# SyncE's transfers in the program's order, the first tables behind a GpSimd copy, bias rows that don't overlap

## The chip, the core and the metric

One core of a Trainium2 chip runs the whole program. It has TensorE (PE, matmuls into PSUM), VectorE (DVE), ScalarE (ACT), GpSimd (POOL) and SyncE (SP); each takes its instructions in the order in which they stand in its queue. SP and POOL here issue most transfers (DMAs) between the large memory and the core's own memory (SBUF); 16 DMA engines carry them. The metric is device time of one execution in microseconds.

## The reference

Three blocks follow one another on a tensor x of 4 x 3072 x 256 in float32.

```
X = rfft(x, axis=1)                       # over the 3072 positions
Yr = Xr @ w_r - Xi @ w_i + b_r ;  Yi = Xr @ w_i + Xi @ w_r + b_i
Yr, Yi = soft_threshold(Yr, 0.01), soft_threshold(Yi, 0.01)
y = irfft(Yr + 1j*Yi, n=3072, axis=1)

x_prev = y shifted by one position (first row zero)
xk = mu_k*y + (1-mu_k)*x_prev ;  xr = mu_r*y + (1-mu_r)*x_prev
z = sigmoid(xr @ w_r2) * (relu(xk @ w_k)**2 @ w_v)     # 256 -> 1024 -> 256

h = z @ w_in ;  out = (h * clip(h+3, 0, 6) / 6) @ w_out   # 256 -> 2048 -> 256
```

## The kernel before

Each float32 operand is split into a rounded high part (ACT copies it, line 147) and a remainder (DVE subtracts, line 148), and three matmuls per product (line 156) keep the precision.

The transform is done as 96 x 32. For batch b there are four stages. `s1(b)` has eight steps: each takes two chunks of x (96 partitions x 512 numbers, line 255), multiplies them by a 96 x 96 table `f1`, copies the sums out of PSUM on ACT (`s1sb`, line 290) and stores them to a scratch tensor `sc_a` (line 291). `mid(b)` has 12 groups j: `s2(j)` reads a chunk of `sc_a` and multiplies by a table `tt` (for j = 0 also by `tex`), `mix(j)` applies `w_r` and `w_i` (held in `aw`), adds `bias` and applies the threshold on DVE (lines 361 to 363), `ia(j)` goes back by another table and stores to `sc_b` (line 379). `ib(b)` has eight steps: they read `sc_b`, multiply by `fi` and store to `sc_y` (line 426). Chunks go through a ring of five buffers `a`; `fetch` splits up to four chunks ahead of their use and loads up to four ahead of the split. Tables come through `load_t` (line 310) on POOL's queue, into three buffers.

Then come 24 tiles of 512 positions of the second block: `load_y` loads a tile `yt` (line 489), `prep` mixes it with its shifted copy by `mus` and `omu` (lines 506 and 511), then the units `u_r`, `u_k`, `u_v`. These tiles are interleaved with the transform of later batches through `feed`. The third block follows, again in 24 tiles. Weights are loaded in pieces by `load` (line 181) and decoded on ACT and DVE in small steps by `decoder`.

The order of the work at the start is a list of parts in `first`: `s1` of batch 0 (steps 0 to 7 of the enumeration at line 814), two steps of `s1` of batch 1 (8 and 9), `mid` of batch 0 (10 to 33), five more steps of `s1` of batch 1, and two steps of `ib` of batch 0. After step 7 the loop loads `w_r` and `w_i`, the second table, and calls `vectors`, which loads the bias and the two mu vectors and computes `omu = 1 - mu`.

The tile framework keeps the order of the program text on the engines that are in the set `order` (line 126). Before, that set names PE, ACT, DVE and POOL; SP's instructions are put in an order by the framework's planner.

The bias tile is 128 partitions x 3 x 256: partition rows 0 to 63 take b_r three times, 64 to 127 b_i three times, and then row 64, slot 0, is written again with b_r (line 476).

Of the kernel before, what the change touches and what calls it, by code (L numbers as in the profile page):

```python
# [9 lines left out]
F32 = mybir.dt.float32  # L10
# [4 lines left out]
ALU = mybir.AluOpType  # L15
# [3 lines left out]
B, S, D = 4, 3072, 256  # L19
# [84 lines left out]
def fourier_mix_ffn_kernel(  # L104
# [18 lines left out]
):  # L123
    nc = tc.nc
    EN = mybir.EngineType
    order = {EN.PE, EN.Activation, EN.DVE, EN.Pool}

    dram = ctx.enter_context(tc.tile_pool(name="dram", bufs=1, space=DRAM))
    sc_a = [dram.tile([N1, N2, D], F32, name=f"sc_a{b}") for b in range(B)]
# [7 lines left out]
    cst = ctx.enter_context(tc.tile_pool(name="cst", bufs=1))  # L137
# [4 lines left out]
    def ptile(name):  # L142
        return ps.tile([128, 1024], F32, tag="h", name=name)
# [6 lines left out]
    def three(o, pairs, first=True, last=True, **kw):  # L150

        n = 3 * len(pairs)
        i = 0
        for (lh, ll), (rh, rl) in pairs:
            for a, c in ((lh, rh), (ll, rh), (lh, rl)):
                nc.tensor.matmul(o, a, c, start=first and i == 0, stop=last and i == n - 1, **kw)  # L156
                i += 1
# [70 lines left out]
    with tc.manual_schedule(engines=order):  # L228
# [6 lines left out]
        mus = cst.tile([128, 2, 2], F32, name="mus")  # L235
        omu = cst.tile([128, 2, 2], F32, name="omu")
        half = cst.tile([128, 1], F32, name="half")
        top = cst.tile([128, 2, 1], F32, name="top")
        bias = fp.tile([128, 3, D], F32, name="bias")
        tex = fp.tile([128, 2, 64], F32R, name="tex")  # L240
# [28 lines left out]
        def take(n):  # L269

            u = head["use"]
            load_chunks(u + n)
            split_chunks(u + n)
            r = [live.pop(u + i) for i in range(n)]
            head["use"] = u + n
            return r

        def fetch():

            split_chunks(head["use"] + 4)  # L280
            load_chunks(head["split"] + 4)

        def s1(b, lo, hi):
            for s in range(lo, hi):
                p = ptile("s1")
                flat = lambda t: t.rearrange("p n d -> p (n d)")
                for i, (h, l) in enumerate(take(2)):
                    three(p[:N1, 512 * i : 512 * i + 512], [((f1[:, 0], f1[:, 1]), (flat(h), flat(l)))])
                sb = fp.tile([128, 4, D], F32, tag="ev", bufs=3, name="s1sb")
                nc.scalar.activation(flat(sb[:N1]), p[:N1], AF.Copy)  # L290
                nc.sync.dma_start(out=sc_a[b][:, 4 * s : 4 * s + 4], in_=sb[:N1])
                if s == 7:
                    ready.add(("a", b))
                    if b == 0:
                        nc.gpsimd.dma_start(out=tex, in_=ext)
                        load_t(0, 0)
                fetch()
                yield
# [4 lines left out]
        def load_t(b, j):  # L303

            if j >= NP + 2:
                b, j = b + 1, j - NP - 2
            if b < B:
                t = fp.tile([128, 2, 640], F32R, tag="t", bufs=3, name="tt")
                c = slice(0 if j < NP else 384, 640 if j >= 2 else 384)
                nc.gpsimd.dma_start(out=t[:, :, c], in_=tab[j, :, :, c])  # L310
                tt[b, j] = t
# [125 lines left out]
        def plan(kind, b, lo=0, hi=0):  # L437
            if kind == "s1":
                v = x[b].rearrange("(p n) d -> p n d", n=N2)
                chunks.extend((v[:, 2 * c : 2 * c + 2], None, N1) for c in range(2 * lo, 2 * hi))  # L440
                return kind, s1(b, lo, hi)
            if kind == "mid":
                v = sc_a[b].rearrange("(j g c) n d -> j (c n) g d", g=2, c=4)
                chunks.extend((v[j], ("a", b), 128) for j in range(NP))
                return kind, mid(b)
            for c in CHUNKS[lo:hi]:
                chunks.extend((sc_b[b][:, n : n + 2], ("b", b), N1) for n in (4 * c, 4 * c + 2))
            return kind, ib(b, lo, hi)
# [22 lines left out]

        def vectors():
            for i, v in enumerate((b_r, b_i)):
                rows = v.partition_broadcast(64).unsqueeze(1).to_broadcast([64, 3, D])
                nc.sync.dma_start(out=bias[64 * i : 64 * i + 64], in_=rows)
            nc.sync.dma_start(out=bias[64:65, 0], in_=b_r.partition_broadcast(1))
            with nc.allow_non_contiguous_dma(reason="two vectors"):
                for i, m in enumerate((mu_k, mu_r)):
                    nc.sync.dma_start(out=mus[:, i], in_=m.rearrange("(a p) -> p a", p=128))
            nc.vector.tensor_scalar(omu, mus, -1.0, 1.0, op0=ALU.mult, op1=ALU.add)  # L480


        seq = [(b, t) for b in range(B) for t in (1, 2, 3, 4, 5, 0)]
# [314 lines left out]
        def stream(parts):  # L798

            for kind, part in parts:  # L800
                if kind == "ib":
                    if ends:
                        for _ in range(2):
                            ends.pop(0)()
                            yield
                        for _ in range(3):
                            fetch()
                            yield
                for _ in part:
                    if ends:  # L810
                        ends.pop(0)()
                    yield

        for step, _ in enumerate(stream(first)):
            if step == LOAD_MIX:
                plain = [(w, w.load(stage1, *job[1:]), job[1:]) for w in aw for job in w.jobs]
                load_t(0, 1)
                vectors()
            if step in SPLIT_MIX:
                w, staged, job = plain.pop(0)  # L820
                for _ in w.decode(staged, *job):
                    pass
            if step == LOAD_FI:
                nc.gpsimd.dma_start(out=fi.rearrange("p s n -> p (s n)"), in_=small[:, 2 * N1 : 4 * N1])
            if step in DECODE:
                next(loads, None)
# [159 lines left out]
```

## Time and profile before

| what | value |
|---|---|
| median of 3 runs | 2081.03 us (2080.89 to 2084.46) |
| the profiled execution | 2082.47 us, span 2080.7 us |
| TensorE busy | 1992.8 us, 96% of the span |
| VectorE, ScalarE busy | 1549.8 us, 1323.2 us |
| mean granted clock | 0.976 of full speed |

The profiled execution lasts 1.77 us longer than the span of its trace, and 1.44 us longer than the median of the runs. Busy time is a sum over stages: a stage in which TensorE works all the time and the start, in which it often waits, are in the same number, so the rows below go by stretches of the span.

### The profile page before, as it was taken

Reading aid. Unit: us, or ns where it says so; the run is one execution under the profiler, and the core shown is the slowest. Engines: PE = TensorE matmul, PEld = TensorE weight load, DVE = VectorE, ACT = ScalarE, POOL = GpSimd, SP = SyncE. Lnnn points to the kernel's source line nnn. Section 1 sums busy time; section 2 is a strip of 40 time slices with the busy share of each in tenths; the row PEclk is TensorE's granted clock in tenths of the full one; section 3 lists DMA queues with packets and bytes.
Section 4 is the critical chain, followed back from the end, with each engine's and each line's share of the span. In section 5 each row is a group of like instructions: output and inputs, shape, how many; then the busy total and the mean of one; then the engine's idle time right before and its main releaser. Section 6 shows DMA issues by size and latency. Waiting matters only on the chain.

```text
span 2080.7 us, 33798 instructions
## 1 busy us (share of the span) xinstructions
PE 1992.8 (96%) x13928; PEld 1844.5 (89%) x13928; DVE 1549.8 (74%) x1975; ACT 1323.2 (64%) x1917; POOL 35.0 (2%) x63
## 2 busy tenths in 40 slices
PE   6878999999999999889998999999999999999998
PEld 4867998898789888667787999999999999999998
DVE  3868667777677686767777777877787778777875
ACT  5556447555754565555646777777777777667775
POOL 0000000000000000000000000000000000000000
PEclk7978999999999999999999999999999999999999
DMA  9765447543653352122100001100110011001100
GB/s 265 240 205 165 123 114 228 163 142 115 216 170 111 95 179 65 63 75 77 51 31 24 29 23 29 32 21 23 30 32 21 22 31 32 21 22 31 32 11 21
DMA packets 106988, 175.85 MB, mean 85 GB/s; under 512 B 12945, under 2 KB 63314, under 8 KB 106834
## 3 DMA queue, kind: packets, MB, share of 16 engines
q1 hardware_dynamic: 96034, 141.76, 22.1%
q0 software_dynamic: 10480, 31.67, 5.7%
q8 instruction: 109, 1.79, 0.4%
q14 instruction: 45, 0.37, 0.1%
q10 hardware_dynamic: 320, 0.26, 0.0%
HBM read 110.35 MB, written 63.31 MB: 83 GB/s over the span
## 4 chain that ended last, share of the span: by engine, by line
PE 76%; DVE 14%; ACT 6%; issue 2%; DMA 2%; SPq 0%; ACTq 0%; DVEq 0%
PE oacc L776 24%; PE rq L776 15%; PE acc L156 8%; PE pk L156 7%; PE cc L776 6%; PE mix L156 5%; PE s L156 4%; DVE g L552 2%; DVE gl L553 2%; PE pr L156 2%; DVE xf L511 1%; PE ia L156 1%; DVE kl L518 1%; PE ib L421 1%; PE ib L420 1%
## 5 line engine op out<-in xcount | busy, mean ns | idle before, releaser
L776 PE MATMUL oacc<-wo_hi,gl 128*128 128x256 f32 x1536 | 426.7, 278 | 0.6 <-DVE gl L750 0.6
L776 PE MATMUL oacc<-wo_hi,gh 128*128 128x256 f32 x1536 | 427.1, 278 | 0.0
L776 PE MATMUL oacc<-wo_lo,gh 128*128 128x256 f32 x1536 | 425.4, 277 | 0.0
L776 PEld LDWEIGHTS oacc<-wo_hi,gl 128*128 128x128 f32 x1536 | 288.7, 188 | 1.0 <-DVE gl L750 0.8
L776 PEld LDWEIGHTS oacc<-wo_hi,gh 128*128 128x128 f32 x1536 | 288.5, 188 | 0.2
L776 PEld LDWEIGHTS oacc<-wo_lo,gh 128*128 128x128 f32 x1536 | 288.7, 188 | 0.0
L732 DVE TENSOR_TENSOR c<-rq,s 128x512 f32<-128x512 f32 x184 | 127.3, 692 | 184.2 <-ACT s L728 184.2
L745 DVE SCALAR_TENSOR_TENSOR g<-g,c 128x1024 f32<-128x1024 f32 x184 | 225.5, 1226 | 27.1 <-ACT g L744 17.4
L749 ACT ACTIVATE gh<-g 128x1024 fp32r<-128x1024 f32 x184 | 195.2, 1061 | 55.8 <-DVE g L745 55.8
L750 DVE TENSOR_TENSOR gl<-g,gh 128x1024 fp32r<-128x1024 f32 x184 | 223.7, 1216 | 1.2 <-ACT gh L749 1.2
L776 PE MATMUL rq<-th,sw 128*128 128x256 f32 x1104 | 217.4, 277 | 7.3 <-DVE g L606 7.3
L744 ACT ACTIVATE g<-c,half 128x1024 f32<-128x1024 f32 x184 | 211.5, 1150 | 4.1 <-DVE c L733 1.4
L712 ACT ACTIVATE s<-rq 128x512 f32<-128x512 f32 x184 | 109.9, 598 | 112.0 <-PE rq L776 111.5
L776 PEld LDWEIGHTS rq<-th,sw 128*128 128x128 f32 x1104 | 166.4, 188 | 7.5 <-DVE g L606 7.5
L156 PE MATMUL acc<-gl,wv_hi 128*128 128x512 f32 x384 | 153.8, 400 | 13.3 <-DVE gl L553 13.3
L547 ACT ACTIVATE g<-pk 128x1024 f32<-128x1024 f32 x96 | 97.6, 1016 | 106.5 <-PE pk L156 106.4
L156 PE MATMUL pk<-kh,wk_hi 128*128 128x512 f32 x384 | 152.8, 398 | 9.3 <-ACT kh L517 5.2
L776 PE MATMUL rq<-tl,sw 128*128 128x256 f32 x552 | 153.9, 279 | 2.8 <-DVE tl L679 2.8
L148 DVE TENSOR_TENSOR al<-a,ah 96x512 fp32r<-96x512 f32 (+1 forms) x176 | 114.9, 684 | 55.2 <-ACT ah L147 55.2
L156 PE MATMUL acc<-gh,wv_hi 128*128 128x512 f32 x384 | 153.2, 399 | 1.6 <-ACT gh L551 1.5
L156 PE MATMUL acc<-gh,wv_lo 128*128 128x512 f32 x384 | 152.2, 396 | 0.0
L156 PE MATMUL pk<-kl,wk_hi 128*128 128x512 f32 x384 | 151.9, 396 | 0.0
(150 smaller groups left out, 4953.0 us busy)
## 6 DMA issues: line engine op xcount, KB each, us to landing
tt<-in_tab_dram POOLq DMA_DIRECT2D x40, 640.0 KB, 4.9
yt<-sc_y SPq DMA_DIRECT2D x23, 608.0 KB, 3.9
a<-in_x_dram SPq DMA_DIRECT2D x64, 192.0 KB, 3.5
sc_a<-s1sb SPq DMA_DIRECT2D x32, 384.0 KB, 3.9
a<-sc_a SPq DMA_DIRECT2D x48, 256.0 KB, 3.2
sc_b<-iasb SPq DMA_DIRECT2D x48, 256.0 KB, 4.8
a<-sc_b SPq DMA_DIRECT2D x64, 192.0 KB, 3.1
sc_y<-ysb SPq DMA_DIRECT2D x32, 384.0 KB, 2.9
```

What stands on the lines that cost most here:

```text
L148: nc.vector.tensor_sub(l, src, h.bitcast(F32))
L156: nc.tensor.matmul(o, a, c, start=first and i == 0, stop=last and i == n - 1, **kw)
L547: nc.scalar.activation(g, p, AF.Relu)
L552: nc.vector.tensor_mul(g, g, g)
L553: nc.vector.tensor_sub(l, g, h.bitcast(F32))
L712: nc.scalar.activation(s[:, 1:3].rearrange("p a n -> p (a n)"), rq, AF.Copy)
L732: nc.vector.tensor_add(c[:, 1::2], two(rq), s[:, 0:2])
L744: nc.scalar.activation(g, c, AF.Relu, bias=half, scale=1.0 / 6.0)
L745: nc.vector.scalar_tensor_tensor(g, g, 1.0, c, op0=ALU.min, op1=ALU.mult)
L749: lambda: nc.scalar.activation(h, g, AF.Copy),
L750: lambda: nc.vector.tensor_sub(l, g, h.bitcast(F32)),
L776: return lambda: nc.tensor.matmul(o, lhs, rhs, start=start, stop=stop, skip_group_check=True)
```

## The change

It edits five places.

1. SP joins the set `order`, so its transfers are issued in the order of the program text, in the whole kernel.
2. In step 4 of `s1` of batch 0, POOL copies one number of the step's output `s1sb` into a new tile `hold`. In POOL's order this copy stands ahead of the transfers of `tex` and of the first three tables, and behind that of `f1`.
3. The bias is written in four transfers that don't overlap: slots 1 and 2 of the two halves, then slot 0 of rows 0 to 64 with b_r and of rows 65 to 127 with b_i.
4. `omu` is computed at step 20 of the enumeration, not in `vectors` (after step 7).
5. As an effect of 1, SP's transfers that the planner had put earlier or later (the loads of `w_r` and `w_i`, pieces of later weights, the zero column of `sc_y`, chunks, `yt`) stand where the text has them.

```diff
-    order = {EN.PE, EN.Activation, EN.DVE, EN.Pool}
+    order = {EN.PE, EN.Activation, EN.DVE, EN.Pool, EN.SP}
...
+        hold = cst.tile([1, 1], F32, name="hold")
...
                 nc.sync.dma_start(out=sc_a[b][:, 4 * s : 4 * s + 4], in_=sb[:N1])
+                if (b, s) == (0, 4):
+
+                    nc.gpsimd.tensor_copy(hold, sb[:1, 0, 0:1])
                 if s == 7:
...
         def vectors():
             for i, v in enumerate((b_r, b_i)):
-                rows = v.partition_broadcast(64).unsqueeze(1).to_broadcast([64, 3, D])
-                nc.sync.dma_start(out=bias[64 * i : 64 * i + 64], in_=rows)
-            nc.sync.dma_start(out=bias[64:65, 0], in_=b_r.partition_broadcast(1))
+                rows = v.partition_broadcast(64).unsqueeze(1).to_broadcast([64, 2, D])
+                nc.sync.dma_start(out=bias[64 * i : 64 * i + 64, 1:3], in_=rows)
+
+            nc.sync.dma_start(out=bias[0:65, 0], in_=b_r.partition_broadcast(65))
+            nc.sync.dma_start(out=bias[65:128, 0], in_=b_i.partition_broadcast(63))
...
-            nc.vector.tensor_scalar(omu, mus, -1.0, 1.0, op0=ALU.mult, op1=ALU.add)
...
             if step == LOAD_FI:
+                nc.vector.tensor_scalar(omu, mus, -1.0, 1.0, op0=ALU.mult, op1=ALU.add)
                 nc.gpsimd.dma_start(out=fi.rearrange("p s n -> p (s n)"), in_=small[:, 2 * N1 : 4 * N1])
```

## Rows read from the trace of the kernel before

**Rows 1.** The page, busy time and share of each engine.

```profile
PE 1992.8 (96%) x13928; PEld 1844.5 (89%) x13928; DVE 1549.8 (74%) x1975; ACT 1323.2 (64%) x1917; POOL 35.0 (2%) x63
```

**Rows 2.** Windows of 50 us: busy by engine, granted clock, DMA share, GB/s.

```profile
0.00:50.00 50.00, 29.34 (x91) 18.81 (x92) 16.76 (x31) 26.08 (x38) 3.90 (x10) 0.79 0.93 260
50.00:100.00 50.00, 43.65 (x342) 41.91 (x342) 44.50 (x73) 26.67 (x44) 5.24 (x9) 0.97 0.79 244
...
200.00:250.00 50.00, 50.00 (x319) 45.22 (x319) 39.31 (x51) 25.52 (x35) 2.11 (x4) 1.00 0.45 133
```

**Rows 3.** Chain of the first 300 us: start, length, what ran or landed.

```profile
4.92 9.52 DMA a<-in_x_dram
...
31.15 8.21 DMA bias<-in_b_i_dram
...
43.57 7.78 PE s L156 x35
...
137.69 2.51 DMA a<-sc_b
```

**Rows 4.** Timeline of SP's queue, 0 to 400 us: start, length, transfer issued.

```profile
3.06 0.43 SPq L181 DMA_DIRECT2D stw<-in_w_r_dram  x1
...
9.86 0.31 SPq L291 DMA_DIRECT2D sc_a<-s1sb  x1
...
27.78 2.51 SPq L291 DMA_DIRECT2D sc_a<-s1sb  x2
...
33.37 2.24 SPq L255 DMA_DIRECT2D a<-sc_a  x4
39.38 0.30 SPq L476 DMA_DIRECT2D bias<-in_b_r_dram  x1
...
334.69 0.38 SPq L489 DMA_DIRECT2D yt<-sc_y  x1
```

**Rows 5.** Short windows: busy by engine, granted clock, DMA share, GB/s.

```profile
5.00:10.00 5.00, 4.07 (x10) 2.75 (x11) 2.03 (x3) 2.45 (x4) 0.00 (x0) 1.00 1.25 315
10.00:15.00 5.00, 2.46 (x7) 1.25 (x5) 0.69 (x1) 0.83 (x2) 0.00 (x0) 1.00 1.13 305
...
25.00:30.00 5.00, 4.17 (x15) 1.88 (x14) 2.83 (x5) 4.48 (x7) 0.00 (x0) 1.00 1.00 339
...
35.00:40.00 5.00, 0.00 (x0) 0.00 (x0) 0.00 (x0) 0.00 (x0) 0.00 (x0) 0.60 0.97 210
...
45.00:50.00 5.00, 5.00 (x25) 5.00 (x25) 1.15 (x3) 1.17 (x2) 0.54 (x1) 0.50 0.90 270
...
127.50:130.00 2.50, 2.39 (x8) 1.95 (x9) 1.45 (x3) 2.50 (x5) 0.06 (x1) 0.50 0.81 257
```

**Rows 6.** Timeline of all engines, with the idle time before each group.

```profile
2.46 1.96 POOL L310 DMA_DIRECT2D tt<-in_tab_dram  x3
...
15.20 0.88 PE L156 MATMUL s<-ah,f 96*96 96x512 f32 x2 [2.75 <-ACT ah L147]
...
40.08 1.36 ACT L147 ACTIVATE ah<-a 128x512 fp32r<-128x512 f32 x2 [7.88 <-DMA a<-sc_a]
...
42.69 0.17 DVE L480 TENSOR_SCALAR omu<-mus 128x4 f32<-128x4 f32 x1 [10.60 <-DMA mus<-in_moe_mu_r_dram]
...
127.52 0.80 PE L156 MATMUL ia<-yh,tt 128*128 128x256 f32 x2 [4.49 <-ACT yh L147]
```

**Rows 7.** The page, DMA issues: KB each, median us to landing.

```profile
a<-in_x_dram SPq DMA_DIRECT2D x64, 192.0 KB, 3.5
...
a<-sc_a SPq DMA_DIRECT2D x48, 256.0 KB, 3.2
```

**Rows 8.** Timeline of ACT, 330 to 360 us.

```profile
344.81 1.02 ACT L290 ACTIVATE s1sb<-s 96x1024 f32<-96x1024 f32 x1 [0.37 <-PE s L156]
...
354.89 1.32 ACT L506 ACTIVATE xf<-yt,omu 128x512 f32<-128x512 f32 x2
```

**Rows 9.** The tile view of yt, all its 23 loads.

```profile
DMA to landing us min/median/max: 3.8/3.9/6.1
```

## Prediction

> **What bounds the kernel now.** I read the page first. TensorE is busy for 1992.8 of 2080.7 us [rows 1], so about 88 us are left to win, and the question is where they lie. The windows of 50 us answer it: TensorE works 29.34 us of the first 50, 43.65 of the next, and all of 200 to 250 [rows 2]. From about 200 us on the kernel hangs on TensorE; SP's order can only cost something there. From 50 to 100 DVE is the busiest with 44.50 us: the first `mid` hangs on DVE and ACT, which take turns, and not on a transfer. So a gain of this change must come out of the first 45 us, and be passed on by what follows.
>
> Next I read the chain of the first 300 us. Three of its links stand where the change works: a chunk of x that takes 9.52 us to land, the bias of 8.21 us, and `s2` that gets going only at 43.57 us [rows 3]. The timelines show who stands still. TensorE waits 2.75 us before 15.20; ACT waits 7.88 us until 40.08 for the first chunk of `sc_a`; DVE waits 10.60 us until 42.69 for the mu vectors, with the remainder of that same chunk queued behind [rows 6]. SP's rows say why: the row 64 of the bias overlaps the two earlier bias transfers, and so its issue comes only at 39.38, and mu's behind it [rows 4].
>
> The sum is made against the profiled execution: 2080.7 us of span plus 1.77 us around it, 2082.47. The median of the runs lies 1.44 us below that, and I take the same difference off both.
>
> **Held-back tables and x first (edits 1 and 2).** Before, POOL issues three tables from 2.46 us on [rows 6], and SP the two 256 KB weights at 3.06, ahead of x's later chunks [rows 4]. By the tile shapes the tables and `tex` are 1.51 MB, the weights 0.52 MB. DMA is at share 1.25 and 1.13 from 5 to 15 us [rows 5], and the chunk asked for at 4.92 takes 9.52 us, against a median of 3.5 [rows 3, 7]. Without the 2.03 MB it should land by about 8.5 us. TensorE then has work without a break up to step 7 of `s1`: the hole of 2.75 us [rows 6] goes. In exchange the text puts two x chunks, which the planner had issued earlier, behind the store of step 0 (9.86 [rows 4]). They would land at about 10.3 + 3.5 = 13.8 us. Six matmuls of 0.44 us make a step of 2.6 us [rows 6]; the hole begins at 12.45, in the middle of the third step, so without it the fourth step starts at about 13.7. Only its second half, from 15.0, needs one of these chunks, so I cost this at nothing.
>
> But the tables come back. Step 4 is the fifth: its matmuls end at about 18.9 and ACT's copy near 20 us, POOL copies its number, and 1.51 MB start beside steps 5 to 7. There DMA is already full: share 1.00, 339 GB/s, from 25 to 30 us [rows 5]. At that rate the tables are 4.5 us of DMA time, of which the weights that have gone give back 1.5. So this part is worth at most 2.75 us, and at worst 2.75 - (4.5 - 1.5) = -0.25. Step 7's store does not have to wait for all the tables, and POOL's transfers share the engines with SP's. I take the middle, 1.5 us.
>
> **Bias behind the chunks, without overlap (edits 1 and 3).** Step 7's store is issued by 30.29, and the four chunks of `sc_a` at 33.37, when it has landed [rows 4]. They queue behind 384 KB of bias; in 35 to 40 us DMA is busy for 0.97 of the time and moves only 210 GB/s [rows 5]. The first chunk is used 6.71 us after its issue [rows 4, 6]. In the text's order the chunks come first, then `w_r` and `w_i`, then the bias. A chunk of `sc_a` takes 3.2 us in the median [rows 7], and at 137.69 the first of four loads issued together landed in 2.51 [rows 3]. I take 3.3, a gain of 3.4 us. The bounds are 4.2 us (6.71 - 2.51) and 0 (the weights and the tail of the tables do to the chunks what the bias did).
>
> What is now later is covered. `w_r` and `w_i` go out about 2.3 and 2.8 us after the first chunk; `mix(0)`, the first reader, has to wait for 7.78 us of matmuls [rows 3] that begin 4.7 us after it. Even the worst landing seen, 9.52, ends at 12.3 us against 12.5. Without that cover ACT, which takes `w_r` in its order ahead of the copy behind `s2(0)`, would hold TensorE some 2.3 us. The bias goes out up to 5.5 us after the first chunk and lands 8.2 later at its old speed, just ahead of its first reader behind `mix(0)`; each us by which it is late is a us on DVE.
>
> **`omu` later (edit 4).** ACT's copy of the first chunk ends half of 1.36 us after 40.08, at 40.76 [rows 6]. The remainder on DVE takes 0.70 us (42.69 + 0.17 + 0.70 is the 43.57 at which TensorE gets going [rows 3, 6]), so it could be done at 41.46. That is 2.1 us. At step 20 `omu` costs its 0.17 us on the engine that sets the pace there; 1.9 us are left. The copy on POOL is one number on an engine that is busy for 35.0 us in all [rows 1], with nothing but those tables behind it; it costs nothing itself.
>
> **SP's order after that (edit 1).** While TensorE is always busy [rows 2] no order can win. Pieces of weights and chunks come later than the planner had them, but each is still asked for two calls or four chunks ahead of its use. The tightest I found is `yt`. The planner issued one at 334.69 [rows 4]; in the text it stands behind the store of the step copied at 344.81 and two chunk loads, so at about 346.7. It lands after 3.9 us, at most 6.1 [rows 9], at 350.6 to 352.8; ACT reads it at 354.89 [rows 8]. So 2.1 us are left at the worst, and I cost this at nothing.
>
> **Sum:** 1.5 + 3.4 + 1.9 = 6.8 us. 2082.47 - 6.8 = 2075.7 for the profiled execution, 2074.2 for the median. `mid(0)` is a chain of compute that moves as a whole, so I pass the gain on in full.
>
> **The rivals.** *The tables take more than they give.* The Trainium skill, "DMA: Bandwidth & Descriptors", section on queues, rings and completion order, says that each DMA engine goes round-robin between the queues that have work for it. The slow x chunk beside POOL's tables fits that rule [rows 3]. As a mechanism of this kernel: POOL's 1.51 MB would take half of the engines for 8.9 us (3.02 MB at 339 GB/s), SP's stores and last chunks come 4.5 us late, and this part is 2.75 - 4.5 = -1.75. For it speaks the full DMA of 25 to 30 us; against it, that x's loads are all issued by then. The gain is 3.4 + 1.9 - 1.75 = 3.5 us, the time 2077.5, no measurable change. The same holds if weights or bias are late by some 3 us.
>
> *SP stands at a store while a load behind it is needed.* Under the text's order a `yt` load that lands more than 8.2 us after its turn (354.89 - 346.7) stops ACT and the units behind. About six of the 23 loads lie beside `s1` and `ib` steps of later batches; late by 2 us each beyond that they cost 12 us, and with the gain of 6.8 the time is 2086. Against it speak the landings of 6.1 at most.
>
> *TensorE keeps its clock.* Before, it stands idle to 43.57 and is then granted 0.50 of full speed, 1.2 GHz instead of 2.4 [rows 5]. With 3.4 and 1.9 us gained its wait is 5.3 us shorter. If it kept 2.4 GHz, the 7.78 us would be 3.9, the gain 10.7 and the time 2070.3. Against it: after an idle time of 4.49 us at 127.52 it was granted 0.50 as well [rows 5, 6].
>
> **How the numbers follow.** A measurement of this kernel tells a change of about 0.2%, 4.2 us, from none. The forecast gets 0.60, the clock 0.07, both faster; the tables 0.21, the same; SP's order 0.12, slower. The terms' bounds give -0.25 + 0 + 1.9 = 1.7 to 2.75 + 4.2 + 1.9 = 8.9 us of gain, and TensorE's clock 10.7; so 2069 to 2080 holds the forecast, the clock and the tables, and leaves out SP's order and some of the tails.
>
> **What would show it.** Right: no hole of TensorE near 12 to 15 us; tables issued near 20 us; the first `sc_a` chunk used some 4 us after its issue; no wait of DVE for mu; `s2` going by about 37 us; the same matmuls some 7 us earlier at 200 us. Wrong: x chunks or stores that land in 6 us or more between 20 and 30 us; ACT waiting for `w_r`, or DVE for the bias; TensorE idle past 200 us with ACT waiting for `yt` or a chunk.

## The result, and the profile after

The changed kernel takes 2111.03 us in the median (2105.00 to 2113.74, 4 runs) against 2081.39 us before: ratio 1.0135, 95% interval 1.0111 to 1.0160. It is 1.35% slower; 2074.2 us was forecast. The profiled execution takes 2109.68 us, with a span of 2107.5 us.

The page's busy times answer to [rows 1]. TensorE has 28.1 us more with the same 13928 matmuls; the other engines stay as they were.

```profile
PE 2020.9 (96%) x13928; PEld 1871.0 (89%) x13928; DVE 1549.8 (74%) x1975; ACT 1322.2 (63%) x1917; POOL 35.0 (2%) x64
```

So the loss is not idle time. The tile view of `rq`, one kind of matmul of the third block (in 23 of its 24 tiles), says where it lies (count: duration min/median/max in ns, first to last start in us). Before:

```profile
L776 PE MATMUL rq<-th,sw x1104: 274/280/580, 1101.4 to 2065.4; 128*128 128x256 f32 x184
```

After:

```profile
L781 PE MATMUL rq<-th,sw x1104: 278/282/582, 1104.1 to 2092.7; 128*128 128x256 f32 x184
```

Counted by these matmuls, the block begins 2.7 us later and lasts 988.6 us instead of 964.0: 24.6 of the 26.8 us of span are lost between its first and its last of these matmuls, where the prediction looked for nothing. One window of 900 us inside it (columns as in [rows 2]), before and after:

```profile
1150.00:2050.00 900.00, 900.00 (x7761) 900.00 (x7760) 701.03 (x837) 642.16 (x970) 0.00 (x0) 1.00 0.09 26
```

```profile
1150.00:2050.00 900.00, 900.00 (x7577) 900.00 (x7576) 687.13 (x821) 626.18 (x948) 0.00 (x0) 1.00 0.09 25
```

In both TensorE never waits, its granted clock is 1.00 (2.4 GHz) and DMA is all but quiet at a share of 0.09. Yet 7577 matmuls run instead of 7761: 118.8 ns from one to the next instead of 116.0. Nobody is late; the same matmuls go slower. "x7761 in 900 us" is the number to follow below.

The start is a second, smaller story. Lines of the timeline of all engines after the change, which answer to [rows 4, 6]:

```profile
14.94 0.70 PE L156 MATMUL s<-ah,f 96*96 96x512 f32 x2 [0.86 <-ACT ah L147]
...
19.89 0.17 POOL L295 COPY hold<-s1sb 1x1 f32<-1x1 f32 x1 [17.98 <-ACT s1sb L291]
20.01 0.56 POOL L299 DMA_DIRECT2D tex<-in_ext_dram  x1
...
20.57 1.96 POOL L314 DMA_DIRECT2D tt<-in_tab_dram  x3
...
30.74 0.63 ACT L147 ACTIVATE ah<-a 96x512 fp32r<-96x512 f32 x1 [4.57 <-DMA a<-in_x_dram]
...
35.69 1.93 SPq L256 DMA_DIRECT2D a<-sc_a  x4
...
38.55 1.36 ACT L147 ACTIVATE ah<-a 128x512 fp32r<-128x512 f32 x2 [3.22 <-DMA a<-sc_a]
...
39.97 0.42 PE L156 MATMUL s<-tt,al 128*128 128x64 f32 x1 [0.31 <-DVE al L148]
...
49.11 0.58 SPq L181 DMA_DIRECT2D stw<-in_moe_w_r_dram  x1
...
58.10 0.43 DVE L196 TENSOR_SCALAR stt<-stw 128x512 uint32<-128x512 uint32 x1 [8.52 <-DMA stw<-in_moe_w_r_dram]
...
58.70 0.69 DVE L365 TENSOR_TENSOR yf<-mix,bias 128x512 f32<-128x512 f32 x1 [0.18 <-issue]
```

Read from the top: the hole of 2.75 us has shrunk to 0.86. The tables start near 20 us, and ACT then waits 4.57 us for a chunk of x. The first chunk of `sc_a` is used 2.86 us after its issue, and `s2` gets going at 39.97 instead of 43.57 [rows 3]. Then DVE stands for 8.52 us at a piece of `moe_w_r`, the first weights of the second block, and the threshold's first `yf` comes at 58.70. In the kernel before it came at 55.11:

```profile
53.11 0.42 DVE L196 TENSOR_SCALAR stt<-stw 128x512 uint32<-128x512 uint32 x1
...
55.11 0.69 DVE L361 TENSOR_TENSOR yf<-mix,bias 128x512 f32<-128x512 f32 x1 [1.59 <-PE mix L156]
```

So 3.6 us gained at `s2` are a loss of 3.6 us some 19 us later. The chain that ended last in the start of the changed kernel has both links, the chunk and the piece:

```profile
22.34 8.32 DMA a<-in_x_dram
...
32.31 3.25 DMA sc_a<-s1sb
...
40.80 7.82 DMA bias<-in_b_i_dram
49.11 8.97 DMA stw<-in_moe_w_r_dram
```

### The profile page after: what moved, and what is told of

It is laid out like the page before. It is cut to its first block, busy times and chain, and to the rows that moved or that the text cites. A ratio compares the mean times of both kernels' runs of the same rounds, so it can differ in the third digit from the quotient of the medians.

```text
span 2107.5 us, 33770 instructions
## 1 busy us (share of the span) xinstructions
PE 2020.9 (96%) x13928; PEld 1871.0 (89%) x13928; DVE 1549.8 (74%) x1975; ACT 1322.2 (63%) x1917; POOL 35.0 (2%) x64
## 4 chain that ended last, share of the span: by engine, by line
PE 76%; DVE 13%; ACT 6%; DMA 3%; issue 2%; SPq 0%; ACTq 0%; DVEq 0%; POOLq 0%
PE oacc L781 25%; PE rq L781 16%; PE acc L156 8%; PE pk L156 7%; PE cc L781 6%; PE mix L156 5%; PE s L156 4%; DVE g L557 2%; DVE gl L558 2%; PE pr L156 2%; DVE xf L516 1%; PE ia L156 1%; DVE kl L523 1%; DMA a<-in_x_dram 1%; PE ib L425 1%
## 5 line engine op out<-in xcount | busy, mean ns | idle before, releaser
L781 PE MATMUL oacc<-wo_hi,gl 128*128 128x256 f32 x1536 | 431.6, 281 | 0.2 <-DVE gl L755 0.2
L781 PE MATMUL oacc<-wo_lo,gh 128*128 128x256 f32 x1536 | 431.4, 281 | 0.0
L781 PE MATMUL rq<-th,sw 128*128 128x256 f32 x1104 | 221.7, 282 | 7.4 <-DVE g L611 7.4
```

The source lines that it names most:

```text
L781: return lambda: nc.tensor.matmul(o, lhs, rhs, start=start, stop=stop, skip_group_check=True)
```

## The experiments

Two theories for the third block. One: the four-byte tile `hold` moves other tiles. It stands among the constants `cst`, whose pool lies ahead of the pools on the left side of SBUF (`kb`, `kw`, `sp`); in the compiled programs it takes a slot of 32 bytes, so all left tiles stand 32 bytes higher, while the weights of the third block (`w2`: `wi`, `wo`) stay on the right. The rival: SP's new order, or what it does to the start, slows the block. "Distance" below is how much the left tiles have moved away from their place relative to `w2`.

### The parts of the change

**The whole change without a new tile.** The copy writes into a third column of `top`, which costs no slot.

```diff
-        hold = cst.tile([1, 1], F32, name="hold")
-        top = cst.tile([128, 2, 1], F32, name="top")
+        top = cst.tile([128, 3, 1], F32, name="top")
...
-                    nc.gpsimd.tensor_copy(hold, sb[:1, 0, 0:1])
+                    nc.gpsimd.tensor_copy(top[:1, 2], sb[:1, 0, 0:1])
```

> The whole change, but the copied number goes into a third column of the tile top, which fills no new slot, so that every tile stays where it was before. Theory A: the third block is as fast as before, and only the start counts; the profile after had the first transform some 4 us later at 135 us than before and 0.7 us later at 722, so 2082 to 2086 us. Rival B: the third block stays slow, about 2108 us.

2087.02 us, ratio 1.0025 (1.0015 to 1.0035), and 7761 matmuls in the window:

```profile
1150.00:2050.00 900.00, 900.00 (x7761) 900.00 (x7760) 701.40 (x837) 642.17 (x969) 0.00 (x0) 1.00 0.09 26
```

The slow third block is gone with the tile, while SP's order, the bias, `omu` and the copy are all there. What is left is a loss of 5.5 us; the time is 1 us above the range that was expected.

**Without the copy.** SP's order, bias and `omu` alone; the tables start early, as before.

> The change without hold: SP in the text's order, bias without overlap, omu late, but tables at the start as before, and no tile moved. Theory A: the third block is as before. At the start the tables no longer meet the last chunks of x near 22 us, so step 7 of s1 should be stored about 2 to 4 us earlier than after the change (32.3 us), and the piece of w_r of the second block, which held DVE until 58.1 us, comes earlier by as much: 2079 to 2083 us. If the tables at the start cost as much as those at 20 us, 2083 to 2086. Rival B: about 2106 us.

2081.55 us, ratio 1.0000 (0.9991 to 1.0009). Its timeline:

```profile
32.02 1.93 SPq L255 DMA_DIRECT2D a<-sc_a  x4
...
34.70 1.41 ACT L147 ACTIVATE ah<-a 128x512 fp32r<-128x512 f32 x2 [3.88 <-DMA a<-sc_a]
...
36.11 0.42 PE L156 MATMUL s<-tt,al 128*128 128x64 f32 x1 [0.31 <-DVE al L148]
...
43.34 0.32 SPq L291 DMA_DIRECT2D sc_a<-s1sb  x1
...
45.29 0.46 SPq L181 DMA_DIRECT2D stw<-in_moe_w_r_dram  x1
...
54.98 0.43 DVE L196 TENSOR_SCALAR stt<-stw 128x512 uint32<-128x512 uint32 x1 [9.25 <-DMA stw<-in_moe_w_r_dram]
...
55.59 0.69 DVE L361 TENSOR_TENSOR yf<-mix,bias 128x512 f32<-128x512 f32 x1 [0.19 <-issue]
```

The first chunk is used 2.68 us after its issue, and `s2` gets going at 36.11, 7.5 us earlier than before. All of it is gone at DVE's wait of 9.25 us: `yf` comes at 55.59 against 55.11. SP issues the piece only at 45.29, behind a store of `s1` of batch 1 (43.34). It lands 9.7 us later, in a stretch in which DMA is full (share 1.10 and 1.03, 406 and 377 GB/s), and the decode at line 196 stands in DVE's order ahead of the threshold:

```profile
45.00:50.00 5.00, 5.00 (x45) 5.00 (x45) 0.73 (x1) 0.00 (x0) 0.00 (x0) 1.00 1.10 406
50.00:55.00 5.00, 1.23 (x11) 1.03 (x9) 0.02 (x1) 0.00 (x0) 0.00 (x0) 0.95 1.03 377
```

Against the version above, the copy itself costs 5.5 us: it moves the tables' 1.51 MB from one busy stretch into another, where the last chunks of x and step 7's store are what the rest waits for.

**The first piece of `moe_w_r` early.** The version without the copy, with that piece issued ahead of the bias.

```diff
             if step == LOAD_MIX:
                 plain = [(w, w.load(stage1, *job[1:]), job[1:]) for w in aw for job in w.jobs]
+                next(loads)
                 load_t(0, 1)
                 vectors()
...
-DECODE = tuple(range(9, 13)) + tuple(range(13, 39, 2))
+DECODE = tuple(range(10, 13)) + tuple(range(13, 39, 2))
```

> The change without hold (e4), and one transfer moved: the first piece of the second block's w_r, 512 KB, is issued right behind w_r and w_i and ahead of the bias, not behind the two stores of s1 of batch 1. In e4 s2 went 7.5 us earlier than before (36.1 against 43.6), but DVE then waited 9.25 us until 54.98 for this piece, with the bias addition of mix(0) queued behind it. Theory (the gain at the start was real and this wait took it back): the piece lands by about 42 to 45, the addition starts near 48 instead of 55.6, and the time is 2081.5 - 7 = 2074.5 us. Rival (the gain is lost again later in the first transform or in its hand-over, whatever DVE waits for here): 2080 to 2082 us.

2077.88 us, ratio 0.9975 (0.9966 to 0.9984): faster than both kernels. DVE takes the piece without a wait, and `yf` comes 7.8 us earlier than before:

```profile
34.83 0.47 SPq L181 DMA_DIRECT2D stw<-in_moe_w_r_dram  x1
...
45.72 0.42 DVE L196 TENSOR_SCALAR stt<-stw 128x512 uint32<-128x512 uint32 x1
...
47.30 0.69 DVE L361 TENSOR_TENSOR yf<-mix,bias 128x512 f32<-128x512 f32 x1 [1.17 <-PE mix L156]
```

That is as much as the whole forecast gain, but it doesn't last. The third `yf` comes at 64.98 against 69.51, only 4.5 us earlier, and in between stands a wait of ACT for a chunk of `sc_a` that the kernel before doesn't have. This version, then the kernel before:

```profile
50.77 0.63 ACT L147 ACTIVATE ah<-a 128x512 fp32r<-128x512 f32 x1 [3.13 <-DMA a<-sc_a]
...
64.98 0.68 DVE L361 TENSOR_TENSOR yf<-mix,bias 128x512 f32<-128x512 f32 x1
```

```profile
69.51 0.69 DVE L361 TENSOR_TENSOR yf<-mix,bias 128x512 f32<-128x512 f32 x1
```

No run took that wait away, so its part in the loss is read from the trace alone. The 4.5 us stay to the end of `mid(0)`, and the median of the runs shows 4.1; 2074.5 us was expected of this version, so it misses by 3.4. The span of the profiled execution is 6.9 us shorter, but its 2075.96 us is one of the faster of 11 runs (2073.33 to 2081.01), so the median is the figure to keep.

**Only two tables held, and later.** The version with the early piece, but with `tex` and the first table at the start and the other two tables behind a copy after step 6.

> As e9, but the tables are parted: tex and the first table go at the start, the second and third wait for a copy on GpSimd after step 6 of s1 (into a free column of top, so that no tile moves). If 1.05 MB less at the start close the hole of TensorE near 13 us and if after step 6 they meet only step 7's store: 1 to 3 us faster than e9, about 2072.5 us. If they meet the chunks of sc_a: as e9 or up to 3 us slower.

2079.49 us, ratio 0.9992 (0.9983 to 1.0000): 1.6 us above the version with all tables early, with intervals that touch. Its chain and its timeline show the price: step 7's store, now beside the tables, takes 6.89 us to land, and ACT waits 7.59 us for the first chunk of `sc_a`. In both versions the held tables collided with what came next.

```profile
28.10 6.89 DMA sc_a<-s1sb
```

```profile
38.11 1.30 ACT L147 ACTIVATE ah<-a 128x512 fp32r<-128x512 f32 x2 [7.59 <-DMA a<-sc_a]
```

**The changed kernel once more.**

> The changed kernel once more. e1 has the same places for every tile as the changed kernel, and yet its third block was faster (about 984 us against 989), with other pitches for single pairs (rq<-xh,wi_lo 118 ns against 132). If the places alone set the pitch, this run has again 132 ns there and 2105 to 2114 us. If a second thing differs from execution to execution, the pairs come out otherwise, and the time lies elsewhere in 2098 to 2114.

2107.20 us, ratio 1.0120 (1.0106 to 1.0134), 7578 matmuls in the window. The slow pace belongs to the program, not to one execution.

### The places of the tiles

**A tile alone, in the kernel before.** A tile of 4 bytes that a memset writes and nobody reads puts the left tiles 32 bytes higher.

```diff
         half = cst.tile([128, 1], F32, name="half")
+        pad = cst.tile([1, 1], F32, name="pad")
...
         nc.vector.memset(half, 0.5)
+        nc.vector.memset(pad, 0.0)
```

> The kernel before, with nothing but a tile of 4 bytes set aside between half and top, as hold is; it fills a slot of 32 bytes, so that the tiles of the pools kb, kw and sp start 32 bytes later, while those on the right side (fp, w2) stay. Theory A (the 30 us are the place of the tiles: TensorE's matmuls of the third block follow each other more slowly when the left tiles move by 32 bytes against the right ones): about 2081 + 26 = 2107 us, and the matmuls of the third block start 118 to 119 ns apart, as after the change, and not 116. Rival B (SP's order or the waits that come with it slow the third block): as before, 2081 us.

2099.99 us, ratio 1.0085 (1.0068 to 1.0102), 7615 matmuls. One unused tile costs 18.5 us against the runs of the kernel before beside it (2081.49), less than the 26 that were expected.

```profile
1150.00:2050.00 900.00, 900.00 (x7615) 900.00 (x7614) 688.95 (x825) 628.83 (x951) 0.00 (x0) 1.00 0.09 25
```

**The same with 64 bytes** (`pad` of 1 x 16 numbers).

> The kernel before with a tile of 64 bytes set aside in the same place, so that the left tiles move by 64 bytes. If only the place within 64 bytes counts (theory A, narrow form), the time is that of before, 2081 us. If any move against the right tiles slows the third block, about 2107. Rival B: 2081 us.

2104.13 us, ratio 1.0110 (1.0095 to 1.0125), 7586 matmuls. The rest modulo 64 bytes is that of the kernel before, and it is slow all the same, so this isn't a matter of a tile's own alignment to 64.

**The other side.** The kernel before with a 4-byte tile behind `wo` in `w2`: the weights stand 32 bytes lower, the left tiles stay.

```diff
                     wo = Weights(w2, w_out, 16, D, "wo")
+                    pad = w2.tile([1, 1], F32, name="pad")
+                    nc.vector.memset(pad, 0.0)
```

> The kernel before with a tile of 4 bytes behind wo in the pool w2, so that wi and wo of the third block start 32 bytes earlier and nothing else moves. If the pitch of a matmul hangs on the places of its own two operands, then oacc (with wo) and the matmuls with wi change their pitch, and rq<-th,sw and rq<-tl,sw, whose operands both stay, keep their 115.8 and 117.2 ns; the time moves by up to 20 us, to either side. If it hangs on the places of the left tiles alone, the time is that of before, 2081 us. If a move of any tile changes all of them, rq<-th,sw changes too.

2103.53 us, ratio 1.0106 (1.0090 to 1.0121), 7616 matmuls, as with the left tiles moved up. I also took the mean time from one start to the next for each kind of matmul from the trace's records: it agrees with that of the 32-byte tile on the left within 0.1 ns (`oacc` 117.7, 118.0 and 118.0 ns; before 115.8, 115.0 and 113.8). Other tiles moved, the same distance, the same pace.

**Left down, and both down.** `half` becomes a column of `top`, which takes a slot away: the left tiles stand 32 bytes lower. Then the same with the tile behind `wo` as well, so that all of them stand 32 bytes lower and the distance is that of before.

```diff
-        half = cst.tile([128, 1], F32, name="half")
-        top = cst.tile([128, 2, 1], F32, name="top")
+        top = cst.tile([128, 3, 1], F32, name="top")
+        half = top[:, 2]
```

> The kernel before, with `half` as a third column of `top`: one 32-byte slot less among the constants, so the tiles on the left (kb, kw, sp) stand 32 bytes lower and the weights of the third block on the right stay. No work changes. Theory 'the pace of the third block hangs on the distance between the left tiles and the weights w2 on the right': a distance that no kernel here has had (+32), so another pace than that of the kernel before (433 matmuls in 50 us); if it is like the others that were moved, 2095 to 2108 us. Rival 'only tiles that move up, or a slot more, cost time': 2081.5 us, 433 matmuls in 50 us.

2097.48 us, ratio 1.0078 (1.0063 to 1.0093), 7634 matmuls: a slot less costs about as much as one more. Counted as "distance" is here, this is -32.

> The kernel before with both moves: the left tiles 32 bytes lower (`half` in `top`) and the weights of the third block 32 bytes lower too (a 4-byte tile behind them). Every tile that TensorE reads in the third block stands elsewhere, their distances are those of the kernel before. Theory of the distance: the pace of the kernel before, 433 matmuls in 50 us and 2081.5 us, within 3 us. Rival 'the place itself counts (its multiple of 64 bytes)': all these tiles now begin on a multiple of 64 bytes instead of 32 beyond one, so the pace differs from before, by some 18 to 25 us as in the other kernels with moved tiles.

2081.48 us, ratio 0.9998 (0.9989 to 1.0007). The window:

```profile
1150.00:2050.00 900.00, 900.00 (x7761) 900.00 (x7760) 700.69 (x836) 642.68 (x969) 0.00 (x0) 1.00 0.09 26
```

Two moves that cost 16 and 22 us alone cost nothing together. In these runs it is the distance that counts, not the place.

**The changed kernel with the weights 32 bytes lower**, a distance of 64.

> The changed kernel with a 4-byte tile behind the weights of the third block, which puts these 32 bytes lower: the left tiles stand 32 bytes higher than in the kernel before, the right ones 32 lower. Theory of the distance: 64 bytes between them as in the kernel whose left tiles were moved by 64, so its pace in the third block (about 119.3 ns from one oacc matmul to the next) and some 2103 to 2109 us. Rival 'the place itself': all tiles begin on a multiple of 64 bytes, as in the kernel with both moved down, so the pace of that kernel.

2107.30 us, ratio 1.0120 (1.0103 to 1.0137), 7587 matmuls; the kernel before with a distance of 64 has 7586. The count is as the distance says, though the kinds of matmul share it out otherwise.

**What step repeats.** The version with the early piece, with tiles of 1024, 512, 256 and 128 bytes in `cst`.

> The version with SP's order, bias, omu and the first w_r piece early (2077.9 us), with a tile of 1024 bytes among the constants: the left tiles stand 1024 bytes higher, all with the same remainder at 64 bytes as in the kernel before. Theory of the distance: a distance of its own, so a pace that may be like before or slower, 2078 to 2105. Rival 'only the remainder at 64 bytes counts': the pace of the kernel before, 433 matmuls in 50 us, 2078 us.

> The same with 512 bytes. If the pace repeats at 512 bytes: 2078 us. If only at 1024: 2095 to 2105 us.

> The same with 256 bytes. If the pace repeats at 256 bytes: 2078 us. If only at 512 or more: 2095 to 2105 us.

> The version with the first w_r piece early (2077.9 us) and a tile of 128 bytes among the constants: the left tiles stand 128 bytes higher. If the pace repeats every 128 bytes: 2078 us and 433 matmuls in 50 us. If it repeats only at 256 or more: 2095 to 2105 us.

| distance | median us | ratio (95%) | matmuls in 1150 to 2050 us |
|---|---|---|---|
| 0 | 2077.88 | 0.9975 (0.9966 to 0.9984) | 7762 |
| 1024 | 2076.42 | 0.9976 (0.9966 to 0.9985) | 7761 |
| 512 | 2076.64 | 0.9979 (0.9969 to 0.9989) | 7761 |
| 256 | 2077.56 | 0.9983 (0.9974 to 0.9992) | 7761 |
| 128 | 2095.67 | 1.0074 (1.0059 to 1.0089) | 7615 |

The pace is back at 256 bytes and its multiples and lost at 128. The windows of 256 and of 128:

```profile
1150.00:2050.00 900.00, 900.00 (x7761) 900.00 (x7760) 700.08 (x836) 643.08 (x970) 0.00 (x0) 1.00 0.09 26
```

```profile
1150.00:2050.00 900.00, 900.00 (x7615) 900.00 (x7615) 689.03 (x825) 628.99 (x951) 0.00 (x0) 1.00 0.09 25
```

**SP's order with the 32 bytes, without the copy.** The changed kernel has 7577 matmuls, the kernel before with a 4-byte tile 7615, although in the compiled programs all tiles stand at the same places. This version has SP's order and the unused tile, and no copy on POOL.

> SP's order, bias and omu as in the change, no copy on GpSimd (the version of 2081.5 us), and a 4-byte tile that nothing but a memset uses: the left tiles stand 32 bytes higher, as in the changed kernel and as in the kernel before with a pad. Theory 'distance alone, the same pace for the same places': the pace of the kernel before with a pad (oacc 117.7, 118.0, 118.0 ns apart), about 2100 us. Rival 'the order of SP's transfers shapes the pace too': the pace of the changed kernel (117.5, 118.2, 118.8), about 2103 us.

2105.98 us, ratio 1.0122 (1.0107 to 1.0137), 7577 matmuls, and the mean from start to start of each kind is that of the changed kernel within 0.02 ns (`oacc` 117.5, 118.2, 118.8). So the second difference, 900 x (7615 / 7577 - 1) = 4.5 us, comes with the rest of the change (SP's order, the bias and `omu` together), not with the copy. Which of the three it is no run tells apart. At distance 0 they make no difference (7761 with them and without), and at 64 none in the count (7587 and 7586). Why they count at 32 stays open.

```profile
1150.00:2050.00 900.00, 900.00 (x7577) 900.00 (x7576) 686.23 (x821) 627.61 (x947) 0.00 (x0) 1.00 0.09 25
```

## Why the prediction was wrong

**The step that failed** is the last sentence on `omu`: the copy on POOL "costs nothing itself". As work it does cost nothing (0.17 us at 19.89). But it needed a place for its number, and I costed the instruction and not its tile. The tile moved everything on the left by 32 bytes against the weights on the right. The version with the tile and without the copy shows the price: ratio 1.0122 against 1.0000 without the tile, 24.9 us against the runs beside it; 18.5 of them are seen in the kernel before, the rest comes with SP's order, the bias and `omu` together. That is most of the 29.6 us of loss. No rival had it either, since all of them stayed in the start or in transfers.

**"No order can win" while TensorE is always busy, and so nothing after 200 us but a late load can cost time.** That reading of [rows 2] was too strong. A window with TensorE busy for all its 50 us shows that it never stands idle, not how fast its matmuls follow one another; the number in brackets behind the busy time does.

**Held-back tables, costed at +1.5 us: wrong in sign.** The hole shrank from 2.75 to 0.86 us, but the lower bound of -0.25 counted the tables as DMA time alone. The x chunk asked for at 22.34 took 8.32 us to land and ACT waited 4.57; `sc_a` was asked for at 35.69 instead of 33.37 [rows 4], so this part measures -2.3 us there. That is 3.7 us later than without the copy (32.02); at the end the copy costs 2087.02 - 2081.55 = 5.5 us, and where the rest of these is lost was not traced. The first rival had the mechanism, with -1.75 us for this part, and a sign that the prediction had named for being wrong came true: an x chunk that lands in 6 us or more between 20 and 30 us. The slow chunk beside POOL's tables bears the rival out; no run here shows how the engines shared themselves between the queues.

**Bias behind the chunks, +3.4, and `omu`, +1.9: right.** The first chunk is used 2.86 us after its issue in the changed kernel and 2.68 without the copy; 3.3 was said. DVE no longer waits for mu. Without the copy `s2` gets going 7.5 us earlier, more than the 5.3 of these two terms, since the four chunks are also asked for 1.35 us earlier and the first lands sooner than was said.

**"I pass the gain on in full": wrong, for a wait that the prediction had looked at and costed at nothing.** It said of pieces of weights that each "is still asked for two calls ... ahead of its use", and named `yt` as the tightest. The tightest was the first piece of `moe_w_r`: asked for at 45.29 and needed by DVE at about 45.7, when `s2` comes earlier. Before it was asked for at 45.36 and taken at 53.11 without a wait, because DVE itself came so late:

```profile
45.36 0.46 SPq L181 DMA_DIRECT2D stw<-in_moe_w_r_dram  x1
```

An earlier `s2` turned slack into a wait of 9.25 us. Issued at 34.83 the piece costs nothing, and the first `yf` is 7.8 us earlier; but after the next wait, 3.13 us for a chunk of `sc_a`, 4.5 of them are left. So `mid(0)` does not move as a whole when only its start comes earlier.

**The other rivals.** In the changed kernel loads of `yt` land too late only twice, for 1.6 us in all. What comes nearest to the second rival is the piece of `moe_w_r`, which stood behind a store when it was needed, but in the start and not at `yt`. TensorE did not keep its clock, as said: from 40 to 45 us it works without a break and is granted 0.50 (1.2 GHz), as in [rows 5]. The changed kernel:

```profile
20.00:25.00 5.00, 4.69 (x12) 2.63 (x11) 2.38 (x4) 3.65 (x6) 2.52 (x5) 0.50 1.03 310
25.00:30.00 5.00, 3.31 (x8) 1.68 (x7) 0.89 (x2) 1.17 (x2) 0.00 (x0) 0.69 1.05 321
...
40.00:45.00 5.00, 5.00 (x24) 5.00 (x24) 2.62 (x4) 2.63 (x4) 0.00 (x0) 0.50 1.03 210
```

The first two rows are the tables' burst: DMA at 1.03 and 1.05, TensorE at 3.31 of 5 us in the second, where it had 4.17 before [rows 5]. TensorE's granted clock was lower there too, 0.50 and 0.69 against 0.76 and 1.00 before, so part of the delay of `s1` can be slower matmuls; ACT's wait of 4.57 us ends at a DMA. The first of these windows before:

```profile
20.00:25.00 5.00, 4.65 (x14) 2.58 (x14) 2.33 (x4) 4.32 (x7) 0.00 (x0) 0.76 0.96 326
```

## What to carry to other kernels

A new tile is an edit of every place behind it: before a change is judged by its instructions, compare the number of matmuls in a long window in which TensorE is always busy, and if it differs, keep the distances of the big tiles, or move them by whole 256 bytes, the step at which the pace came back here. A transfer that is brought forward is worth what the next wait leaves of it, so list every load by when its reader will come after the gain, not by when it came before. Bulk that is held back from one full stretch of DMA has to be carried in another; of the two places tried here both cost time, so hold it only into a stretch that has room and no store that is waited for.

## What the runs showed of the hardware

With the granted clock at 1.00 and no wait in the profile, matmuls of 256 columns followed one another every 116.0 ns or every 117.9 to 118.8 ns, depending on the distance between tiles on the two sides of SBUF. Distances of 0, 256, 512 and 1024 bytes gave the fast pace; 32, 64, 128 and -32 gave slower ones.

By the same mean from start to start, the matmuls `rq<-th,sw` slowed from 115.8 to 118.2 ns when only `w2` had moved, although both of their own operands stayed where they were. So it isn't only the two operands of one matmul that are in each other's way; matmuls near them in TensorE's order read `w2`. Which two reads meet (TensorE's rows and weights, or those of DVE and ACT, which work beside it) no run here tells apart.

The Trainium skill, "TensorE: Matmul & The Clock Gate", section "Step-by-step: what each phase is for", says that TensorE reads the streaming operand and the weights through two SBUF read ports of their own, so that loading the next tile's weights takes no read bandwidth from the running matmul. No run here shows whether these two reads meet. What the runs show is that a move of 32 bytes on one side, with the work of the third block as it was, cost 16 to 22 us of 2081 in the kernel before, so places are not free here, whatever the ports.
